# A planner that holds VectorE's work back for GpSimd's casts: linear attention and an expert layer on one core

## The chip, the cores and the metric

One core of one Trainium2 chip runs the kernel. The metric is the device time of one execution in microseconds (us). Each kernel has one profiled execution; of the others only the time, the span and the mean granted clock are on record. SBUF and PSUM are the two memories in which the kernel's tiles lie; its matmuls write PSUM. Engines: PE is TensorE's matmul side, PEld its weight loads, DVE is VectorE, ACT is ScalarE, POOL is GpSimd, SP is SyncE, which here issues loads.

## The reference

```python
def phi(x):                                   # ELU + 1
    return np.where(x > 0, x, np.exp(x) - 1.0) + 1.0
# q, k, v: 8 x 8 x 576 x 64 fp32
kv  = einsum('bhsd,bhse->bhde', phi(k), v);   z   = phi(k).sum(2)
num = einsum('bhsd,bhde->bhse', phi(q), kv);  den = einsum('bhsd,bhd->bhs', phi(q), z) + 1e-6
x = (num / den) transposed and reshaped to 4608 x 512
P = exp(x @ w_gate - max)                     # 8 experts, then 8 rounds of sinkhorn scaling of P
out = sum over e of P[:, e:e+1] * (relu(x @ w1[e]) @ w2[e])      # w1: 512 x 1024, w2: 1024 x 512
```

## The kernel before

The attention is cut into 16 head groups. A group loads k, q and v, casts q and v to fp16 on GpSimd, makes phi of k on ScalarE (exponential) and VectorE (minimum, add, maximum), multiplies kv, transposes q on TensorE, makes phi of q, and then divides, transposes and multiplies on. Matmuls of the first expert fill TensorE between these small steps. This mixed part is called the front here.

No instruction order of the front is written down. Tasks with estimated durations go to a list scheduler inside the kernel, the planner. It picks at every step the task that can start first, and so decides the order on each engine (and for some tasks the engine). In the built program each engine's instructions stand in that fixed order, and those that need another engine's result wait for it by semaphore. Durations in the planner are thus guesses that only shape the order.

```python
class _Plan:
    def add(self, eng, fn, deps=(), prio=0.0, acq=(), use=(), lat=0.0, after=0.0, stall=0.0):
        ...
    def run(self):
        def slot(t):
            r = t["ready"]
            ...                      # and when the buffers that the task takes come free
            return r
        while left:
            ...                      # te, e, t: the task that can start first, and its engine
            t["done"] = te + t["eng"][e] + t["lat"]
            free[e] = te + max(0.0, t["eng"][e] - self.OVER.get(e, 0.0))
            if t["stall"]:
                free["dve"] = max(free["dve"], te) + t["stall"]     # flat charge for a GpSimd cast
            ...
            t["fn"](e)               # emits the instructions

p_in = {n: S_.pool(2) for n in "kvq"}         # two input buffers each for k, q, v
...
def copy(e, dst, src):
    if e == "act":   nc.scalar.copy(out=dst, in_=src)
    elif e == "dve": nc.vector.tensor_copy(out=dst, in_=src)
    else:            nc.gpsimd.tensor_copy(out=dst, in_=src)

# cast of q to fp16 (v likewise)
tqq = fadd(QE[n] if n < 2 else ("pool", 1.2), f_q, ..., stall=QS[n] if n < 2 else 0.35)

def f_m(_):                                    # phi of k on VectorE: the "e" and "tk" instructions
    nc.vector.tensor_scalar(out=ge["tile"], in0=ge["tile"], scalar1=1.0, scalar2=None, op0=ALU.min)
    o = gt["k"]["tile"].rearrange("p j r d -> p r j d")
    if gt["k"]["on"] == "act":
        nc.vector.tensor_tensor(out=o, in0=o, in1=ge["tile"], op=ALU.max)
    else:
        for r in range(2):
            nc.vector.scalar_tensor_tensor(out=o[:, r], in0=gin["k"]["tile"][:, r], scalar=1.0,
                                           in1=ge["tile"][:, r], op0=ALU.add, op1=ALU.max)
tph["k"] = fadd(("dve", 1.35), f_m, deps=[te, tt_], use=[ge, gt["k"], gin["k"]], prio=pr)

def f_qm(_, ...):                              # phi of q on VectorE: the "eq" and "qpT" instructions
    nc.vector.tensor_scalar(out=m, in0=m, scalar1=1.0, scalar2=None, op0=ALU.min)
    nc.vector.scalar_tensor_tensor(out=gq["tile"][...], in0=gp["tile"][...], scalar=1.0,   # gp is in PSUM
                                   in1=m, op0=ALU.add, op1=ALU.max)
tq.append(fadd(("dve", 0.25 + 0.165 * w), f_qm, deps=[t2, tqa], use=[gp, geq, gq], prio=pr))
```

The softmax here doesn't subtract the row's maximum and nothing guards it: scores larger than these inputs give would overflow.

## Time and profile before

| what | before |
|---|---|
| time, median of 3 runs (range) | 985.96 us (984.77 to 986.05) |
| span of the profiled run, its granted clock | 981.6 us, 0.997 (its time was 983.43 us, below all three above) |
| PE busy, idle in the whole span | 964.9 us, 16.7 us |
| PE idle from 20 to 125 us | 5.93 us |
| last logits of the front start at | 138.65 us |
| first matmuls on the gathered rows (xs) start at | 194.76 us |

In the timeline views a line reads: start, length, engine, source line, operation, output<-inputs, shapes, count; in square brackets the idle time of that engine just before, and what ended it.

### The profile page before, as it was taken

The page shows a single profiled execution, that of the slowest core. Times are in us where ns is not written, and L with a number is a line of the kernel's source. Part 1 is how long each engine was busy: PE and PEld are TensorE (multiplying, and loading weights), DVE is VectorE, ACT ScalarE, POOL GpSimd, SP SyncE. Part 2 cuts the span into 40 slices and gives each one's busy share as a digit, 9 for nine tenths or more (in the row PEclk, how much of TensorE's full clock was granted, in tenths as well). Part 3 has the DMA queues.
Part 4 walks back from the last instruction along what each step waited for, and adds up shares of the span by engine and source line. Part 5 has one row for each costly group of instructions (what it writes and reads, how often), then busy time and mean ns, then how long its engine had stood idle before and what let it go on. Part 6 is the DMA issues. An engine that isn't in the chain of part 4 may idle for free.

```text
span 981.6 us, 21435 instructions
## 1 busy us (share of the span) xinstructions
PE 964.9 (98%) x8716; PEld 793.0 (81%) x8716; DVE 767.9 (78%) x1541; ACT 559.6 (57%) x1056; POOL 143.8 (15%) x185
## 2 busy tenths in 40 slices
PE   8998999999999999999999999999999999999997
PEld 4555654488888888888888888888888888888885
DVE  6888788777777777777777777777777777777774
ACT  5787754755555555555555555555555555555552
POOL 5333200001111111111111111111111111111110
PEclk9999999999999999999999999999999999999999
DMA  9976785062226322272226322272225322236654
GB/s 302 308 262 229 224 212 210 1 128 76 74 77 142 96 75 76 75 161 76 76 76 138 100 76 75 77 162 76 76 76 134 104 76 76 76 108 163 161 157 101
DMA packets 47027, 121.98 MB, mean 124 GB/s; under 512 B 4176, under 2 KB 18000, under 8 KB 46928
## 3 DMA queue, kind: packets, MB, share of 16 engines
q1 hardware_dynamic: 32128, 99.76, 30.7%
q0 software_dynamic: 14480, 20.33, 11.6%
q8 instruction: 68, 1.11, 0.5%
q10 hardware_dynamic: 320, 0.52, 0.1%
q14 instruction: 31, 0.25, 0.1%
HBM read 119.69 MB, written 17.69 MB: 140 GB/s over the span
## 4 chain that ended last, share of the span: by engine, by line
PE 89%; DVE 5%; ACT 3%; DMA 2%; issue 1%; SPq 0%; DVEq 0%; ACTq 0%
PE ye L840 33%; PE hq L655 23%; PE att L655 11%; PE Zye L655 6%; PE Zye L840 6%; PE ye L734 4%; PE hq L564 4%; DVE qpT L362 1%; DMA kin<-in_k_dram 1%; DVE tk L300 1%; PE kv_ps L324 1%; DVE eq L361 1%; DMA xd<-xT 1%; PE xt_ps L415 0%; PE num_ps L399 0%
## 5 line engine op out<-in xcount | busy, mean ns | idle before, releaser
L854 DVE SCALAR_TENSOR_TENSOR acc<-ye,P_sb,acc 128x256 f32<-128x256 f32 x620 | 264.6, 476 | 95.2 <-PE ye L840 78.0
L655 PEld LDWEIGHTS <-W 128*128 128x128 f16 x2016 | 197.0, 98 | 23.8
L840 PEld LDWEIGHTS <-S 128*128 128x128 f16 x1984 | 194.1, 98 | 22.5
L840 PE MATMUL ye<-T,S 128*128 128x256 f16 x1488 | 192.9, 273 | 0.0
L864 POOL TENSOR_TENSOR acc<-acc,st 128x256 f32<-128x256 f32 x124 | 87.5, 725 | 625.4 <-ACT st L861 620.5
L681 ACT ACTIVATE h<-hq 128x512 f16<-128x512 f32 x126 | 76.5, 607 | 161.9 <-PE hq L655 161.9
L655 PEld LDWEIGHTS <-w 128*128 128x128 f16 x1512 | 147.5, 98 | 23.3 <-issue 1.0
L840 PEld LDWEIGHTS <-h 128*128 128x128 f16 x1488 | 145.6, 98 | 16.8
L655 PE MATMUL hq<-xs,W 128*128 128x256 f16 x1008 | 151.2, 273 | 0.0
L655 PE MATMUL att<-xs,W 128*128 128x256 f16 x1008 | 151.1, 272 | 0.0
L655 PE MATMUL hq<-xs,w 128*128 128x256 f16 x1008 | 140.8, 272 | 0.8 <-DVE h L684 0.8
L813 DVE TENSOR_TENSOR S<-h 128x1024 f16<-128x1024 f16 x124 | 85.2, 687 | 57.9 <-ACT h L681 57.9
L684 DVE CUSTOM_DVE_ANT_0 h<-att,s 128x512 f16<-128x512 f32 x126 | 86.6, 687 | 13.0 <-ACT s L671 13.0
L861 ACT ACTIVATE st<-Zye,P_sb 128x256 f32<-128x256 f32 x124 | 52.0, 470 | 78.0 <-PE Zye L840 78.0
L671 ACT COPY s<-hq 128x512 f32<-128x512 f32 x126 | 75.1, 596 | 36.8 <-PE hq L655 36.8
L678 ACT ACTIVATE h<-Zye 128x512 f16<-128x512 f32 x126 | 75.2, 597 | 35.1 <-PE Zye L655 35.1
L684 DVE CUSTOM_DVE_ANT_0 h<-hq,s 128x512 f16<-128x512 f32 x126 | 86.4, 686 | 0.1
L667 ACT COPY Zye<-hq 128x512 f32<-128x512 f32 x126 | 73.2, 581 | 17.4 <-PE hq L655 17.4
L734 PE MATMUL ye<-w,h 128*128 128x512 f16 x320 | 77.6, 379 | 0.3 <-DVE acc L225 0.3
L655 PE MATMUL Zye<-xs,w 128*128 128x256 f16 x504 | 75.6, 273 | 0.0
L675 ACT COPY s<-att 128x512 f32<-128x512 f32 x126 | 74.5, 591 | 0.0
L564 PE MATMUL hq<-xT,w 128*128 128x512 f16 x288 | 70.6, 379 | 1.0 <-ACT h L568 0.9
(90 smaller groups left out, 977.9 us busy)
## 6 DMA issues: line engine op xcount, KB each, us to landing
xs<-xd SPq DMA_DIRECT2D x63, 896.0 KB, 4.6
w<-in_moe_w_dram POOLq DMA_DIRECT2D x14, 1024.0 KB, 11.7
out_dram<-acc SPq DMA_DIRECT2D x68, 128.0 KB, 2.4
kin<-in_k_dram SPq DMA_DIRECT2D x14, 576.0 KB, 5.3
qin<-in_q_dram SPq DMA_DIRECT2D x14, 576.0 KB, 6.3
vin<-in_v_dram SPq DMA_DIRECT2D x14, 576.0 KB, 7.7
xd<-xst SPq DMA_DIRECT2D x9, 512.0 KB, 3.2
xd<-xT SPq DMA_DIRECT2D x9, 256.0 KB, 7.4
```

The source lines that it names most:

```text
L564: nc.tensor.matmul(ghq["tile"], lhsT=gw1["tile"][:, c, ts(f, P)], rhs=xT[:, c, ds(512 * g, 512)], start=(c == 0), stop=(c == NDT - 1))
L655: nc.tensor.matmul(dst[:, p, :], lhsT=lhs(p, c), rhs=rhs(c), start=(first and p == 0 and c == 0), stop=(c == 1), skip_group_check=True)
L671: nc.scalar.copy(out=gs2["tile"], in_=gX["tile"])
L675: nc.scalar.copy(out=gs5["tile"], in_=gR["tile"])
L678: nc.scalar.activation(out=hd(0, 0), in_=Zt[1], func=AF.Relu)
L681: nc.scalar.activation(out=hd(1, 0), in_=gX["tile"], func=AF.Relu)
L684: nc.vector._custom_dve(TENSOR_ADD_SAT, out=dst, in0=ps, in1=sb, s0=3.0e38, s1=0.0)
L734: nc.tensor.matmul(gy[tt]["tile"], lhsT=gh["tile"][:, f, ds(P * tt, P)], rhs=gw2["tile"][:, f, :], start=(f == 0), stop=(f == NFT - 1))
L813: nc.vector.tensor_tensor(out=Sx[:, i], in0=a0, in1=a1, op=op)
L840: nc.tensor.matmul(bank(g_)[:, s, :], lhsT=lhs(s, kk), rhs=rhs(kk), start=(new and s == 0 and kk == 0), stop=(kk == 3), skip_group_check=True)
L854: nc.vector.scalar_tensor_tensor(out=dst(), in0=bank(g_)[:, s, :], scalar=P_sb[:, gg, e:e + 1], in1=dst(), op0=ALU.mult, op1=ALU.add)
L864: nc.gpsimd.tensor_tensor(out=dst(), in0=dst(), in1=gst["tile"], op=ALU.add)
```

## The change

The intent: in place of a flat charge to VectorE for every cast on GpSimd, the planner remembers until when the planned cast on GpSimd runs, and makes the VectorE tasks marked `port=True` (phi of k, phi of q, one early cast of q) wait for it. The rest of VectorE's work may be planned under a cast.

What stands behind the mark is seen in the traces as length alone. In the kernel before, from 20 to 150 us, a tk pair takes 1.43 us by itself and 2.28 to 2.39 where casts cover 1.0 us or more of it (0.58 us of cast over one pair left it at 1.43); e takes 0.40 to 0.46 us and, with 0.6 us or more under a cast, 0.91 to 0.97; eq 0.23 to 0.34 us and, with 0.4 us or more, 0.58 to 1.01; tk by maximum 0.76 us and, with 0.9 us or more, 1.53 and 1.59. The qpT instruction, with one input in PSUM, keeps its 0.82 us even where a cast covers all of it. `port` is the planner's name; "the port" stands for this lengthening, and "port-bound" for e, tk and eq.

```diff
-    def add(self, eng, fn, deps=(), prio=0.0, acq=(), use=(), lat=0.0, after=0.0, stall=0.0):
+    def add(self, eng, fn, deps=(), prio=0.0, acq=(), use=(), lat=0.0, after=0.0, lock=False, port=False):
...
+        locked = [0.0]
+
         def slot(t):
-            r = t["ready"]
+            r = max(t["ready"], locked[0]) if t["port"] else t["ready"]
...
-            if t["stall"]:
-                free["dve"] = max(free["dve"], te) + t["stall"]
+            if t["lock"]:
+                locked[0] = t["done"]
...
-        tqq = fadd(QE[n] if n < 2 else ("pool", 1.2), f_q, ..., stall=QS[n] if n < 2 else 0.35)
+        tqq = fadd(QE[n] if n < 2 else ("pool", 1.2), f_q, ..., lock=n > 1 or QE[n][0] == "pool", port=n < 2 and QE[n][0] == "dve")
...
-        tph["k"] = fadd(("dve", 1.35), f_m, ..., prio=pr)
+        tph["k"] = fadd(("dve", 1.35), f_m, ..., prio=pr, port=True)
...        # the cast of v changes as that of q does
-            tq.append(fadd(("dve", 0.25 + 0.165 * w), f_qm, ..., prio=pr))
+            tq.append(fadd(("dve", 0.25 + 0.165 * w), f_qm, ..., prio=pr, port=True))
```

Nothing is added to the program itself: the same work with the same semaphores, in another order. Source lines in the changed kernel are two higher than before (L300 becomes L302).

More of the change, by code (lines that the diff above doesn't have):

```diff
@@ L37, in add @@
         k = len(self.t)
-        t = {"eng": eng, "fn": fn, "prio": prio, "acq": tuple(acq), "lat": lat, "stall": stall, "kids": [], "nd": 0,
+        t = {"eng": eng, "fn": fn, "prio": prio, "acq": tuple(acq), "lat": lat, "lock": lock, "port": port, "kids": [], "nd": 0,
              "ready": after, "done": None, "id": k}
@@ L229 @@
     w_last, in_prev = [None], [None]
-    VE = [("pool", 1.2), ("pool", 1.2)]; VS = [0.9 if x[0] == "pool" else 0.0 for x in VE]
+    VE = [("pool", 1.2), ("pool", 1.2)]
     QT_ATT, QT_HQ = (1,), ()
-    QE = [("dve", 0.75), ("act", 1.17)]; QS = [0.9 if x[0] == "pool" else 0.0 for x in QE]
+    QE = [("dve", 0.75), ("act", 1.17)]
     front_ids = []
@@ L277, in f_q @@
             copy(e, gt["q"]["tile"].rearrange("p j r d -> p r j d"), gin["q"]["tile"])
-        tqq = fadd(QE[n] if n < 2 else ("pool", 1.2), f_q, deps=[tin["q"]], acq=[gt["q"]], use=[gin["q"]], prio=pr, stall=QS[n] if n < 2 else 0.35)
+        tqq = fadd(QE[n] if n < 2 else ("pool", 1.2), f_q, deps=[tin["q"]], acq=[gt["q"]], use=[gin["q"]], prio=pr, lock=n > 1 or QE[n][0] == "pool", port=n < 2 and QE[n][0] == "dve")
         ge = S_.grp(p_e)
@@ L303, in att @@
         tt_ = fadd({"dve": 0.6, "act": 1.17}, f_t, deps=[tin["k"]], acq=[gt["k"]], use=[gin["k"]], prio=pr)
-        tph["k"] = fadd(("dve", 1.35), f_m, deps=[te, tt_], use=[ge, gt["k"], gin["k"]], prio=pr)
+        tph["k"] = fadd(("dve", 1.35), f_m, deps=[te, tt_], use=[ge, gt["k"], gin["k"]], prio=pr, port=True)
         gvv = S_.grp(p_vv)
@@ L313, in att @@
         tvv.append(fadd(VE[n] if n < 2 else ("pool", 1.2), f_v, deps=[ta, tin["v"]],
-                        use=[gvv, gin["v"]], prio=pr, stall=VS[n] if n < 2 else 0.35))
+                        use=[gvv, gin["v"]], prio=pr, lock=n > 1 or VE[n][0] == "pool", port=n < 2 and VE[n][0] == "dve"))
         vcast[n] = tvv[0]
@@ L366, in att @@
             t2 = fadd(("act", 0.2 + 0.09 * w), f_qe, deps=[t1], acq=[geq], use=[gp], prio=pr)
-            tq.append(fadd(("dve", 0.25 + 0.165 * w), f_qm, deps=[t2, tqa], use=[gp, geq, gq], prio=pr))
+            tq.append(fadd(("dve", 0.25 + 0.165 * w), f_qm, deps=[t2, tqa], use=[gp, geq, gq], prio=pr, port=True))
         js = [0, 2, 4, 6, 7]
```

## The prediction

> **What bounds the kernel now.** I read the page first (engine shares and the slices), then the busy time by stretches, then TensorE's own instructions in order of time with the wait before each, then the same view for VectorE and GpSimd side by side. The page says that TensorE is the bound:
>
> ```profile
> PE 964.9 (98%) x8716; PEld 793.0 (81%) x8716; DVE 767.9 (78%) x1541; ACT 559.6 (57%) x1056; POOL 143.8 (15%) x185
> ```
>
> So a change of order can only win what TensorE idles, or lose by making it idle more. Where it idles, the stretches tell (columns: stretch, its length, then busy time and instructions of each engine, granted clock, DMA share, GB/s):
>
> ```profile
> 0.00:20.00 20.00, 15.96 (x124) 7.76 (x125) 12.70 (x26) 9.53 (x17) 10.95 (x18) 0.91 0.95 282
> 20.00:40.00 20.00, 18.37 (x181) 10.80 (x179) 17.45 (x35) 13.48 (x26) 7.64 (x7) 1.00 1.11 334
> 40.00:60.00 20.00, 19.78 (x224) 12.45 (x222) 18.18 (x36) 17.50 (x33) 8.48 (x7) 1.00 0.93 336
> 60.00:80.00 20.00, 19.54 (x245) 12.15 (x243) 16.81 (x34) 15.63 (x31) 5.69 (x5) 1.00 0.64 222
> 80.00:100.00 20.00, 16.93 (x172) 10.06 (x170) 16.67 (x34) 13.65 (x27) 6.06 (x5) 1.00 0.56 185
> 100.00:115.00 15.00, 14.59 (x162) 8.55 (x160) 10.47 (x24) 12.79 (x26) 3.45 (x3) 1.00 0.62 203
> 115.00:125.00 10.00, 9.86 (x136) 6.67 (x134) 9.38 (x21) 6.16 (x13) 3.82 (x4) 1.00 1.09 284
> 125.00:982.00 857.00, 849.89 (x7493) 724.52 (x7490) 666.19 (x1340) 470.84 (x890) 97.68 (x136) 1.00 0.37 104
> ```
>
> The attention part (the front: 16 head groups mixed with matmuls of the first expert) ends at about 138 us, where the last logits run. TensorE idles 4.0 us in the first 20 us (start-up, waiting for the first loads and casts, partly filled with dummy matmuls), then 1.63 + 0.22 + 0.46 + 3.07 + 0.41 + 0.14 = 5.93 us up to 125 us, and from there to 185 us it has no idle time at all. All that this change can reach is thus about 10 us, 1% of the run; a change over 2% is out of reach upwards.
>
> What the change aims at shows in VectorE and GpSimd in order of time (start, length, engine, instruction):
>
> ```profile
> 41.66 1.15 POOL L227 CAST tq<-qin 128x1152 f16<-128x1152 f32 x1 [2.16 <-DMA qin<-in_q_dram]
> 43.08 1.15 POOL L227 CAST vv<-vin 128x1152 f16<-128x1152 f32 x1 [0.27 <-DMA vin<-in_v_dram]
> 95.92 1.46 POOL L227 CAST tq<-qin 128x1152 f16<-128x1152 f32 x1 [3.17 <-PE qt_ps L352]
> ```
>
> ```profile
> 40.22 1.43 DVE L300 SCALAR_TENSOR_TENSOR tk<-kin,e 128x576 f16<-128x576 f32 x2
> 41.98 1.01 DVE L361 TENSOR_SCALAR eq<-eq 128x640 f16<-128x640 f16 x1
> 43.09 0.82 DVE L362 SCALAR_TENSOR_TENSOR qpT<-qt_ps,eq 128x640 f16<-128x640 f16 x1
> 95.62 2.37 DVE L300 SCALAR_TENSOR_TENSOR tk<-kin,e 128x576 f16<-128x576 f32 x2
> ```
>
> The pair of tk halves takes 1.43 us alone and 2.37 us when the cast of 95.92 falls on it. The minimum on eq (0.26 to 0.33 us elsewhere) takes 1.01 us and ends with the cast of 41.66. But the 43.09 instruction, whose one input is in PSUM, keeps its 0.82 us under a whole cast. Summing length minus usual length over the stretched VectorE instructions after 20 us, from the same list: e (usual 0.45) 0.50 + 0.46 + 0.52; tk pair (1.43) 0.85 + 0.96 + 0.94; tk by max (0.76) 0.83 + 0.77; eq (0.28 to 0.32) 0.50 + 0.70 + 0.39 + 0.65 + 0.26. That is 8.3 us of VectorE. TensorE's waits behind it are far smaller:
>
> ```profile
> 29.19 0.67 PE L324 MATMUL kv_ps<-vv,tk 64*128 64x130 f16 x17 [1.16 <-DVE qpT L362]
> 84.40 0.68 PE L324 MATMUL kv_ps<-vv,tk 64*128 64x130 f16 x17 [0.70 <-DVE qpT L362]
> 98.13 0.39 PE L399 MATMUL num_ps<-kvz,qpT 128*128 128x128 f16 x4 [1.25 <-DVE rden L381]
> ```
>
> [...]
>
> **The change part by part.** Every arithmetic result and transfer stays. The old planner charged VectorE a flat 0.35 us for each later cast by GpSimd (28 of them, 9.8 us), whatever VectorE ran. That sum is close to the 8.3 us seen, so the load was right on average; only its place was wrong. The new planner charges nothing flat and holds back marked tasks (phi of k, phi of q, the early q cast) until the planned cast ends, and lets other tasks go first. No wait is added to the program: only order and choice of engine move.
>
> I compared the built programs' instruction order. TensorE, GpSimd and SyncE have the same instructions; TensorE's order differs only from the first groups to the first sinkhorn steps, and GpSimd swaps a few casts. Before the front closes both run 164 first-layer and 144 second-layer matmuls of the first expert, so what follows the close is the same amount of work and the end should move as the close moves. VectorE gains 8 small kvz copies (8 x 0.22 = 1.8 us), one acc copy (0.68) and one group of tk (1.43 in place of 0.76), and loses two xT copies (2 x 0.45): about +2.2 us. ScalarE loses 1.17 + 8 x 0.21 + 0.59 and gains 2 x 0.64: -2.2 us. With VectorE 85% busy between 20 and 125 us (89.0 of 105), 2.2 us more fits only if stretch goes down by as much.
>
> Now the path, wait by wait. First, the start: the new order puts one kvz copy (0.22) and one xT copy (0.45) on VectorE ahead of the second group's last xn, and lets ScalarE do the next exponential (1.18) before its second xT copy. The first real matmuls start at 22.55 us; I put them some 0.5 us later. At the 29.19 wait, VectorE's order (e, tk, eq, qpT, eq, qpT) is unchanged and the casts beside it come when their loads land, so the stretch stays; and 16 instead of 20 first-layer matmuls stand ahead of that kv. Four of 0.216 us are 0.87 us that TensorE now idles there. With 0.3 us of later start: a loss of 1.2 us by 30 us.
>
> Then, waits behind a stretched VectorE: 0.18 (at 45.86), 0.18 (64.80), 0.24 (82.05), 0.70, 1.25, and 0.21 (111.20): 2.76 us. In the new order other work (xn, acc, xT, kvz copies) stands where the port-bound ones stood. I guess three quarters saved: 2.1 us. The waits on ScalarE or on accumulator copies (0.27, 0.30, 0.40, 0.18) are 1.15 us; ScalarE's lighter load may save 0.3. Sum: +1.2 - 2.1 - 0.3 = -1.2 us, so 986.0 becomes 984.8.
>
> **Rivals.** (a) All waits of the front behind VectorE go and nothing is lost at the start: -2.8 - 1.2 = -4.0, about 982. For it: 8.3 us of stretch to save. Against: VectorE gets 2.2 us more, and the first wait's chain is the same. (b) VectorE's stretch falls, but it now idles or runs 2.2 us more while TensorE waits for phi of k held back: a delayed kv takes the place of a stretched one, and the start's loss stays: +1 to +2, about 987. For it: casts are released by landing loads and freed buffers, not by the plan, so a plan exact to a cast's 1.15 us may miss. (c) Nothing: TensorE has enough filler matmuls and each saved wait comes back at the next join; within 0.5 us of 986. The page's 98% speaks for it.
>
> **Range and chances.** The sum of -1.2 us has errors of about 1 us in the start and 1.5 us in the later waits; the three runs of before already span 1.3 us. So 984.8, with 982.3 to 987.3 for 8 in 10. Over 2% is 19.7 us: faster would need twice all reachable idle time, slower a new stall that nothing here suggests. Faster 0.01, within 2% 0.98, slower 0.01.
>
> **What would show it.** In the changed kernel's trace: tk pairs near 1.43 us more often and summed stretch after 20 us well under 8.3 (about 4); the 98.13 and 84.40 waits gone; the kv wait near 29 us longer, near 2 us; first real matmuls near 23 us; the last logits of the front about 1 us before 138.65; from there to the end the same length within 0.5 us. The prediction is wrong if the close moves by more than 3 us, if the time after the close changes, or if stretch falls while TensorE's idle time does not.

## The result, and the profile after

The changed kernel takes 987.95 us (median of 4 runs, 987.58 to 988.7); the kernel before in the same rounds and the earlier ones 985.37 (4 runs, 984.77 to 986.05). The ratio is 1.0027, with a 95% interval of 1.001 to 1.0044. A ratio here is the mean time of one kernel's runs over that of the other's runs of the same rounds, so it is not quite the ratio of the medians. The two are the same within 2%, but the new one is slower, and 987.95 lies above the stated range (982.3 to 987.3).

The page of the changed kernel, engine shares:

```profile
PE 965.3 (98%) x8716; PEld 792.1 (80%) x8716; DVE 770.7 (78%) x1549; ACT 558.0 (57%) x1048; POOL 143.9 (15%) x185
```

TensorE is as busy as before (965.3 against 964.9 us), but the span grew from 981.6 to 985.7: its idle time went from 16.7 to 20.4 us. (The profiles overstate the difference: the profiled execution of before took 983.43 us, 1.9 less than its median, that of the changed kernel 987.82.) Where, the time windows of the changed kernel tell (columns as in the prediction):

```profile
20.00:40.00 20.00, 17.45 (x172) 9.96 (x170) 16.37 (x34) 13.02 (x23) 7.92 (x7) 1.00 1.12 334
40.00:60.00 20.00, 17.21 (x189) 9.99 (x188) 16.96 (x31) 13.04 (x24) 7.02 (x6) 1.00 0.70 245
60.00:80.00 20.00, 18.02 (x175) 10.27 (x172) 16.69 (x33) 14.99 (x27) 5.24 (x5) 1.00 0.60 216
80.00:100.00 20.00, 19.52 (x265) 12.97 (x264) 17.22 (x37) 16.45 (x33) 6.35 (x6) 1.00 0.56 191
100.00:115.00 15.00, 14.35 (x187) 9.34 (x186) 14.17 (x28) 10.93 (x21) 4.63 (x4) 1.00 0.93 319
...
```

Counting also the window that is not shown (115 to 125 us, 9.93 busy), TensorE idles from 20 to 125 us 2.55 + 2.79 + 1.98 + 0.48 + 0.65 + 0.07 = 8.52 us, where it was 5.93. From 80 to 100 us it gained (3.07 to 0.48); from 40 to 60 and from 60 to 80 it lost more (0.22 to 2.79, 0.46 to 1.98). VectorE, which was to be relieved, is busy 1.2 us less from 40 to 60 us, 16.96 for 18.18, just where TensorE waits for it more. TensorE's own instructions in the changed kernel, those with a long wait before them:

```profile
28.66 0.67 PE L326 MATMUL kv_ps<-vv,tk 64*128 64x130 f16 x17 [1.27 <-DVE qpT L364]
...
51.38 0.21 PE L326 MATMUL kv_ps<-vv,tk 64*128 64x130 f16 x1 [0.87 <-DVE qpT L364]
...
52.85 0.69 PE L326 MATMUL kv_ps<-vv,tk 64*128 64x130 f16 x17 [1.25 <-DVE qpT L364]
...
71.14 0.39 PE L401 MATMUL num_ps<-kvz,qpT 128*128 128x128 f16 x4 [0.80 <-DVE rden L383]
72.24 0.28 PE L401 MATMUL num_ps<-kvz,qpT 128*128 128x128 f16 x2 [0.72 <-DVE xn L406]
```

The two waits that the change was to remove, 0.70 us ahead of 84.40 and 1.25 ahead of 98.13, are gone. In their place stand 0.87 + 1.25 us at the kv of group 4 (ahead of its first matmul and of its other 17) and 0.80 + 0.72 at a group's division: 3.64 us for 1.95. The end of the front, in TensorE's timeline, first of the kernel before and then of the changed one:

```profile
138.65 1.04 PE L433 MATMUL lg_ps<-wg_sb,xT 128*128 128x8 f16 x36
...
194.76 0.60 PE L655 MATMUL hq<-xs,w 128*128 128x256 f16 x4
```

```profile
141.81 1.04 PE L435 MATMUL lg_ps<-wg_sb,xT 128*128 128x8 f16 x36
...
198.04 0.60 PE L657 MATMUL hq<-xs,w 128*128 128x256 f16 x4
```

The last logits come 3.16 us later and the first matmuls on gathered rows 3.28 later. From there to the end are 981.6 - 194.8 = 786.8 and 985.7 - 198.0 = 787.7 us. So some 3.2 of the 4.1 us by which the two profiled spans differ are made in the front.

Last, VectorE and GpSimd side by side in the changed kernel:

```profile
42.58 1.27 POOL L229 CAST vv<-vin 128x1152 f16<-128x1152 f32 x1 [0.30 <-PE qt_ps L354]
...
42.88 2.25 DVE L302 SCALAR_TENSOR_TENSOR tk<-kin,e 128x576 f16<-128x576 f32 x2
...
55.82 1.15 POOL L229 CAST tq<-qin 128x1152 f16<-128x1152 f32 x1 [1.00 <-DMA qin<-in_q_dram]
55.92 1.65 DVE L299 TENSOR_TENSOR tk<-tk,e 128x1152 f16<-128x1152 f16 x1
```

The collisions are still there: 2.25 us for the pair that takes 1.43 alone, 1.65 for the maximum that takes 0.76. The casts beside them took 1.27 and 1.15 us, where most take 1.15. Summed as in the prediction, the stretch (the time by which VectorE instructions are lengthened) after 20 us is 8.7 us, where it was 8.3. For the comparisons below I use one fixed sum over all instructions of the five shapes e, tk (two forms) and eq (two forms), from 20 to 150 us, each against the same usual length; it gives 7.6 us before and 8.0 after, and is called the stretch sum. Its level moves by some tenths of a microsecond with the choice of the usual lengths.

Why did the collisions not go? The planner's own times, printed while it plans, give two reasons. The first is that the plan is off:

```
task                          planned start   started on the chip
phi of k, group 4             40.30           42.39
cast of v, group 5            43.43           42.58
cast of q, group 6            47.98           50.71
```

In the plan phi of k of group 4 (to 41.65) is clear of the cast of v, by 1.8 us. On the chip the cast starts 0.85 us earlier than planned and the phi 2.1 us later, so they meet. The rule works with times to a tenth of a microsecond in a plan that is 1 to 3 us off here, and up to 10 us off by the end of the front.

The second reason weighs more: most of the collisions stand in the plan itself. Since only VectorE is held, the planner starts a cast in the middle of a marked task without objection. The planners of both kernels were run again for all 28 casts of groups 2 to 15. In the changed kernel's plan no marked task of these groups starts inside a cast, as the rule demands, but 16 casts start inside a marked task, 7 of them inside phi of k. In the plan of before, 12 of these tasks start inside a cast, and 11 casts inside such a task. In the changed kernel's trace 16 pairs of a cast and a phi overlap in the phi's e, tk or eq by more than 0.1 us; 11 of the 16 overlap in the plan already. The two pairs shown above are among the other five.

### The profile page after: what moved, and what is told of

The parts are those of the page before. It is cut to its first block, busy times and chain, and to the rows that moved or that the text cites. A ratio compares the mean times of both kernels' runs of the same rounds, so it can differ in the third digit from the quotient of the medians.

```text
span 985.7 us, 21428 instructions
## 1 busy us (share of the span) xinstructions
PE 965.3 (98%) x8716; PEld 792.1 (80%) x8716; DVE 770.7 (78%) x1549; ACT 558.0 (57%) x1048; POOL 143.9 (15%) x185
## 4 chain that ended last, share of the span: by engine, by line
PE 90%; DVE 7%; ACT 2%; issue 1%; DMA 0%; DVEq 0%; ACTq 0%
PE ye L842 33%; PE hq L657 23%; PE att L657 11%; PE Zye L657 6%; PE Zye L842 5%; PE ye L736 5%; PE hq L566 4%; DVE qpT L364 1%; DVE xn L406 1%; DVE tk L302 1%; PE kv_ps L326 1%; DVE tk L299 1%; DVE eq L363 1%; PE num_ps L401 1%; PE xt_ps L417 1%
```

## The experiments

The theory from the two traces was: the collisions are not what changed; the new order holds phi back, has its own waits, and these are the 3 us. Rivals: the stretch itself costs more where it now falls; the transposes of q take, ahead of a kv, the two PSUM buffers that it needs ("banks"); single held-back phis are to blame and can be moved; late k loads; or the whole is chance, since any change of a number in the planner gives another order. Eighteen kernels were run. Two of them give a wrong result; the others are correct.

**1 and 2. Both orders with hardly any cast.** Casts on GpSimd of groups 2 to 15 do 2 of 64 columns. The result is wrong; the order is untouched.

```diff
+            w = 2 if len(tiny) > 1 else src.shape[-1]
+            tiny.append(1)
-            nc.gpsimd.tensor_copy(out=dst, in_=src)
+            nc.gpsimd.tensor_copy(out=dst[:, :, :, 0:w], in_=src[:, :, :, 0:w])
```

> The changed kernel with its order untouched, but GpSimd's casts of groups 2 to 15 copy 2 of each 64 columns (wrong result on purpose)[...]. Theory A (the new order itself keeps TensorE waiting[...]): it stays 2 to 3 us slower than the same edit of the kernel before. Theory B (same quality of order, but casts now fall on worse VectorE instructions): it comes within 0.7 us of that. Both expect stretch near 0 and a time below 987.95.

> The kernel before with the same shortened casts (wrong result on purpose). It gives the most that any avoidance of the port could win: if the port's cost on TensorE is the 2.8 us that I counted, about 982.5; if TensorE's filler hides it, 984 to 985.

Measured: the changed kernel 983.62 us (ratio to before 0.9982, 0.9971 to 0.9994), the kernel before 980.44 (0.9952, 0.994 to 0.9964), with before at 985.04 in the same job. The stretch sum falls to nothing in both (-0.6 and -0.8; below zero, since the usual lengths are a little long). The order's difference stays: 983.62 - 980.44 = 3.2 us, where with casts it was 987.95 - 985.37 = 2.6. The casts cost about as much under either rule: 985.04 - 980.44 = 4.6 us before, 987.95 - 983.62 = 4.3 after; these are upper bounds for what the collisions cost, since the shorter cast itself also ends sooner. In the changed order without casts the new waits are still there:

```profile
50.78 0.21 PE L330 MATMUL kv_ps<-vv,tk 64*128 64x130 f16 x1 [0.74 <-DVE qpT L368]
51.78 0.69 PE L330 MATMUL kv_ps<-vv,tk 64*128 64x130 f16 x17 [0.79 <-DVE qpT L368]
69.53 0.28 PE L405 MATMUL num_ps<-kvz,qpT 128*128 128x128 f16 x2 [0.68 <-DVE xn L410]
```

That is 2.21 us where it was 3.64, with nothing stretched. They belong to the order. In the kernel before without casts, no wait of 0.4 us behind VectorE is left from 20 to 145 us. (TensorE's idle time in these two profiles, 4.98 and 4.61 us from 22 to 150 us, doesn't show the 3.2: the profiled run of before without casts was its slowest, 982.07 against 979.95 to 980.61, and has 1.55 + 0.82 us of waits for weights in it. So the 3.2 us rest on the timings, whose ranges do not touch; the waits show where such a difference can stand, not its sum.)

**3 and 4. The two halves of the change.** The first drops the flat charge and holds nothing back; the second holds back and charges as well.

```diff
 # neither (f_qm likewise)
-tph["k"] = fadd(("dve", 1.35), f_m, ..., prio=pr, port=True)
+tph["k"] = fadd(("dve", 1.35), f_m, ..., prio=pr)
 # both
 if t["lock"]:
     locked[0] = t["done"]
+    free["dve"] = max(free["dve"], te) + 0.35
```

> The changed kernel with the flat charge gone but nothing held back[...]. If dropping the 0.35 us charge per cast is what hurts (VectorE planned too light), it is as slow as the changed kernel or slower, 988 or more. If holding back phi of k and phi of q hurts, it comes back to about 985.5.

> The changed kernel with the flat charge of 0.35 us per cast put back beside the holding. If the lost charge hurts, about 985.5; if the holding hurts, 988 or more (VectorE is then charged twice).

Measured: neither 988.49 (1.003, 1.0018 to 1.0042), both 990.28 (1.0046, 1.0032 to 1.006); each has one half-clock dip of 1.7 us in its profile, of the kind described with runs 13 to 16. With the charge alone (before, 985.37) and the hold alone (after, 987.95) all four combinations are there, one order each: by the time, the charge alone is best. By the front it looks different. The first matmuls on gathered rows start at 195.19 us with both and at 194.76 with the charge alone, but at 198.04 with the hold alone and at 199.55 with neither (1.7 of it the dip). What "both" loses, it loses after the front: TensorE waits 1.16 us for ScalarE ahead of 207.10 and 2.83 ahead of 215.44, and its dip stands there. So the traces point to the lost charge more than to the hold. As other experiments show, one order of a rule is a draw with a spread of several us, so four orders do not divide the cost between the two.

**5. The transposes of group 5 behind the kv of groups 4 and 5.** The recorded order of the changed kernel is replayed task for task (a replay without moves gives identical instruction lists), with three things of group 5 moved: its transposes, exponentials and phi of q.

```diff
 # the recorded task list
-qt5 qe5 ... kv4 kv5 ... qm5
+kv4 kv5 z4 z5 qt5 qe5 ... xn4 qm5
```

> The changed kernel's order replayed instruction for instruction, with one thing moved: the transposes of group 5's q with their exp and phi go behind the kv matmuls of groups 4 and 5, as they stand in the kernel before. Bank theory (held-back phi of q 4 lets the transposes of q 5 take the two PSUM banks that kv 4 needs, 0.87 + 1.25 us of TensorE's idle time): about 2 us under the changed kernel, 985.9. Rival (TensorE meets the same VectorE load at the next join): within 0.7 us of 988.

Measured: 987.74 (1.0027, 1.0015 to 1.0039): 1.8 us above the bank theory's figure, and where the rival put it. The waits at the kv of group 4 went, and in their place came, in TensorE's timeline of this run:

```profile
52.44 0.38 PE L613 MATMUL den_ps<-kvz,qpT 128*128 128x2 f16 x9 [0.33 <-DVE kvz L463]
...
59.27 0.69 PE L562 MATMUL kv_ps<-vv,tk 64*128 64x130 f16 x17 [1.01 <-DVE qpT L600]
```

with smaller ones of 0.28 to 0.29 us ahead of 51.23, 58.05 and 61.46. The next groups pay. This does not clear the PSUM buffers: the waits at group 4 did go with the transposes, but these now stand ahead of the kv of group 6, and its 17 matmuls wait for the second phi of q of group 5 in the same way (the 1.01 us). The bank theory of the one wait fits; that its removal wins time does not.

**6. Also phi of k of group 8 behind the division of group 6.**

```diff
-... m8 ... xn6 ...
+... xn6 m8 ...
```

> The same, and phi of k of group 8 goes behind the division of group 6, which waited behind it (TensorE idle 0.80 + 0.72 us at 71 to 72 us). If each such wait is lost time: another 1 to 1.5 us less, about 984.5. If the waits come back elsewhere: as the run with the first move.

Measured: 988.65 (1.0035, 1.0022 to 1.0049): 4.2 us above the hope; the rival, waits that come back, had it about right. The waits at the division went and two others came, one of 0.86 us ahead of 79.40 and this one:

```profile
74.92 0.40 PE L590 MATMUL qt_ps<-ident,tq 128*128 128x128 f16 x4 [1.73 <-DVE qpT L600]
```

**7. The order of before, phi of k of groups 10 and 12 held back by hand.** This is the improvement for which the change was made: the two waits at 84.40 and 98.13 of before removed and nothing else, by moving one phi of k ahead of each to after the division that it delayed.

> The kernel before, its order replayed, with two moves on VectorE alone: phi of k of groups 10 and 12 go behind the phi of q and the divisions that waited for them (TensorE idle 0.24 + 0.70 and 1.25 us). If TensorE's waits in the front are lost time one for one, 2.2 us under the kernel before, about 982.9. If they come back: within 0.7 us of it.

Measured: 989.47 (987.88 to 992.57; ratio 1.0047, 1.0031 to 1.0063): 6.6 us above the first expectation, and above the second as well. The two waits went, as planned. What came are two waits of the same kind, 2.44 and 2.37 us long, on TensorE (ahead of 88.56 and 113.41) and two of 10.40 and 10.64 us on GpSimd; the first of each, in the timelines of this run:

```profile
88.56 0.17 PE L611 MATMUL den_ps<-kvz,qpT 128*128 128x2 f16 x1 [2.44 <-ACT kvz L459]
```

```profile
96.70 1.15 POOL L463 CAST vv<-vin 128x1152 f16<-128x1152 f32 x1 [10.40 <-DMA vin<-in_v_dram]
```

Phi of k is the last reader of the k input buffer, and there are two. Held back, it frees the buffer late: the k loads of groups 12 and 14 were issued at 88.14 and 106.57 us in place of 81.97 and 98.05. The loads of q and v stand behind that of k in SyncE's order (in this run at 88.60 and 89.11 us, after 88.14), so the casts of both waited, and the stream of the later groups with them. A phi with slack, off the critical path itself, still sets when the next loads start. Something else came with the two long waits: in the profiled execution (992.57 us, the slowest) a dip of the granted clock follows each, 0.68 + 1.00 and 0.76 + 0.96 us of lost clock, 3.4 us in all; such dips are described with runs 13 to 16. The other executions have no such record, so their part in the 6.6 us is not shown.

**8 to 12. Is it the order or the rule?** Four other values of the planner's numbers (the flat charge 0.40 or 0.30 for 0.35, the told length of a cast 1.15 or 1.25 for 1.2) give other orders of the same rule. And one run keeps the changed order but lets GpSimd yield on the chip: before each cast it reads 64 columns of the latest phi's output, so that a cast cannot start inside a phi.

```diff
+            if lastp[0] is not None:                       # set by f_m and f_qm
+                nc.gpsimd.tensor_copy(out=junk, in_=lastp[0])
             nc.gpsimd.tensor_copy(out=dst, in_=src)
```

> The kernel before with its flat charge at 0.40 us in place of 0.35, nothing else. If the order of the kernel before owes its time to that charge being right on average, within 1 us of 985.0. If it owes it to one lucky order among many (its transposes of q 5 again stand ahead of kv 4 here), 987 to 990 as the three re-made orders measured so far.

> The old rule with its charge at 0.30 us in place of 0.35. If the old rule is the better one, 984 to 986, as at 0.35 and 0.40. If orders are draws, 984 to 990.

> The new rule unchanged, but the planner is told that a cast takes 1.15 us (as the trace has it) and not 1.2: a control for chance. If the rule itself costs 2.6 us, 987 to 989. If each re-made order is a draw from a spread of some 2 us either way, it may come out anywhere from 984 to 990.

> The same control to the other side, 1.25 us: 987 to 989 if the rule costs, 984 to 990 if the order is a draw.

> The changed kernel, same order on every engine; before each GpSimd cast GpSimd also reads 64 columns that the latest phi task ahead of it in the plan has written, so it can't start a cast before that task is done, as the plan assumes. If the change fails because casts start earlier on the chip than planned[...]: summed stretch from 8.7 to under 4 us and the time to 985 or less. If the order itself is at fault: stretch falls, time within 1 us of 988 or above, since casts come later.

Measured, charge 0.40: 984.98 (0.9998, 0.9986 to 1.001). Charge 0.30: 981.57 (0.9953, 0.9934 to 0.9972). Cast told as 1.15: 987.21 (1.001, 0.9989 to 1.003). Told as 1.25: 984.96 (0.999, 0.997 to 1.0009). Yielding: 986.88 (1.0008, 0.999 to 1.0027). All but the first of these shared one job, which was noisy: the kernel before lay between 983.4 and 989.26 in it, so their intervals are wide.

The yield did what it was made for: the stretch sum fell from 8.0 to 4.0. It adds on the chip the direction that the planner's rule lacks. What it was worth is at most about 987.95 - 986.88 = 1.1 us (across two jobs, whose ranges touch), and TensorE's idle time from 22 to 150 us even stayed (8.36 for 8.09). The tk pair just ahead of the kv, at 50.90, takes its plain 1.43 us and the kv waits still. TensorE's timeline of the yielding run:

```profile
53.58 0.21 PE L332 MATMUL kv_ps<-vv,tk 64*128 64x130 f16 x1 [0.95 <-DVE qpT L370]
54.58 0.69 PE L332 MATMUL kv_ps<-vv,tk 64*128 64x130 f16 x17 [0.79 <-DVE qpT L370]
```

**13 to 16. More draws of each rule,** to tell the rule from chance: the cast told as 1.18 and 1.22, the charge at 0.37 and 0.25.

> Another draw of the new rule, a cast told as 1.18 us. Rule costs: 987 to 989. Draws: 984 to 990.

> Another draw of the new rule, 1.22 us. Rule costs: 987 to 989. Draws: 984 to 990.

> Another draw of the old rule, charge 0.37 us. Old rule better by itself: 982 to 986. Draws: 982 to 990.

> Another draw of the old rule, charge 0.25 us. Old rule better by itself: 982 to 986. Draws: 982 to 990.

Measured: 995.46 (1.0106, 1.0092 to 1.0119), 993.3 (1.0085, 1.0071 to 1.0099), 982.79 (0.9978, 0.9964 to 0.9993), 982.8 (0.9978, 0.9966 to 0.9991). All draws together; the idle column is 128 us less TensorE's busy time from 22 to 150 us:

| rule | told | median us | stretch sum us | PE idle 22 to 150 us |
|---|---|---|---|---|
| flat charge | 0.25 | 982.8 | 8.8 | 4.78 |
| flat charge | 0.30 | 981.57 | 7.0 | 5.34 |
| flat charge (before) | 0.35 | 985.37 | 7.6 | 5.64 |
| flat charge | 0.37 | 982.79 | 7.7 | 4.84 |
| flat charge | 0.40 | 984.98 | 8.7 | 6.81 |
| hold, no charge | cast 1.15 | 987.21 | 8.0 | 9.20 |
| hold, no charge | cast 1.18 | 995.46 | 8.2 | 14.02 |
| hold, no charge (after) | cast 1.20 | 987.95 | 8.0 | 8.09 |
| hold, no charge | cast 1.22 | 993.3 | 7.8 | 12.43 |
| hold, no charge | cast 1.25 | 984.96 | 8.5 | 6.45 |

The means are 983.5 us for the flat charge and 989.8 for the hold. Of 25 pairs, 23 have the hold above the charge. The mean stretch sum is 8.0 us for the charge and 8.1 for the hold. So the new rule (the hold in place of the charge) reaches nothing of what it is for on average, and makes slower orders: 4.6 us more of TensorE idle time in the mean (10.0 against 5.5), most of the 6.3 us. The worst draw shows the kinds of wait it makes, in TensorE's timeline for the cast told as 1.18:

```profile
54.05 0.69 PE L326 MATMUL kv_ps<-vv,tk 64*128 64x130 f16 x17 [1.70 <-DVE qpT L364]
...
112.92 0.44 PE L417 MATMUL xt_ps<-ident,xn 128*128 128x128 f16 x5 [1.80 <-DVE xn L406]
...
132.55 0.38 PE L377 MATMUL den_ps<-kvz,qpT 128*128 128x2 f16 x9 [2.93 <-ACT kvz L225]
```

And it shows where most of the rest is. The time windows of the same run right after the first of these waits (the third number from the end is the granted clock):

```profile
54.00:56.00 2.00, 1.95 (x27) 1.16 (x28) 0.45 (x2) 0.93 (x3) 1.13 (x1) 0.82 1.03 381
56.00:58.00 2.00, 2.00 (x36) 1.78 (x33) 1.56 (x5) 1.11 (x4) 0.14 (x2) 0.50 0.89 305
```

The granted clock falls to half (0.50 from 56 to 58 us), while TensorE has work without a gap (2.00 us busy of 2.00). Summed over slices of 4 us, (1 - clock) x 4 comes to 0.36 + 1.36 = 1.72 us there, as half speed for 3.44 us would give. The other two waits are followed by the same, 1.36 + 0.36 and 1.12 + 0.60. The cast told as 1.22 has two such dips, 3.4 us, after waits of 1.75 and of 0.94 + 1.83 us; the other eight draws of the table have none from 20 to 960 us. (A dip between 8 and 16 us, during the start-up, stands in 11 of the 20 profiles, of both rules; TensorE is busy 2.0 to 3.9 us in its slices of 4.) In all 20 profiles there are ten dips between 20 and 960 us, of 1.68 to 1.72 us each. Each stands in the 4 us slice in which a TensorE wait ends or in the next one, and these waits are from 0.56 us (run 3, ahead of 111.75) to 2.93 us long. But the 0.87 + 1.25 us of the changed kernel have no dip behind them, while the 0.86 + 0.78 us of run 17 at the same kv do. So these traces do not tell which waits a dip follows. In the profiled executions a dip costs its full size: the start of the first matmuls on gathered rows, less TensorE's idle time since 20 us, less the dips, is 187.3 to 188.7 us in the five profiles with a dip in the front and 186.9 to 188.8 in the others. So the two outliers are waits plus dips. As an estimate, if the dips of the profiled execution stand in the median one too, 995.46 - 5.2 and 993.3 - 3.4 would both be near 990, and without the dips the means of the rules still differ by 6.3 - (5.2 + 3.4) / 5 = 4.6 us, about the idle time. (It is not sure that they do: the execution of 993.3 us has a mean clock of 0.998 over its span of 991.5 us; two dips of 1.7 us would alone bring it to 0.997.) The pair of kernels has no dip in the profiled front after 20 us, so its difference there is idle time alone.

A caution goes with the table: one number told differently is one draw, and the told number differs in kind between the rules. That the single pair of kernels differs by just 2.6 us is chance within that spread; that it differs upwards is what 23 of the 25 pairs do. The ten draws set hold without charge against charge without hold, so they do not tell the two apart either.

**17 and 18. Are late k loads the cause?** In the changed kernel the k loads of groups 10 and 11 are issued at 71.06 and 80.73 us, in the kernel before at 67.29 and 69.87; run 7 had shown that a late k load can cost much. A third k buffer, under the two recorded orders, takes this dependence away. Room was made by cutting a constant tile of zeros from 512 to 64 columns, read repeatedly.

```diff
-gr["tile"] = fp.tile([P, 2, NJ, D], FP32, tag=nm + "in", name=nm + "in", bufs=2)
+gr["tile"] = fp.tile([P, 2, NJ, D], FP32, tag=nm + "in", name=nm + "in", bufs=3 if nm == "k" else 2)
```

> The order of the changed kernel replayed task for task, with nothing else changed but a third buffer for the k input (the room is made by cutting the constant zero tile of the warm-up matmuls from 512 to 64 columns, read repeatedly). Load theory (the new rule holds phi of k back, which frees the two k buffers late, so that loads, casts and everything behind them come late): the load of k no longer waits for phi of k, k loads of groups 6 to 13 are issued 3 us or more earlier than in the changed kernel (59.43, 71.06, 80.73, 97.74), and the time falls from 987.9 to 984 to 985.5. Rival (the waits come from the order in which PE, VectorE and ScalarE take their work, and the loads are late beside it): loads earlier, time stays at 987 to 988.5.

> The control: the order of the kernel before, replayed task for task, with the same third k buffer and the same cut of the zero tile. Load theory: here phi of k frees the buffers early already, so the time gains at most 1 us: 984 to 985.4. Rival: also 984.5 to 986; what tells them apart is the difference between the two orders, which is 2.6 us with two buffers: the load theory expects under 1.2 us with three, the rival 2 to 3 us.

Measured: the changed order 991.13 (1.006, 1.0046 to 1.0073), the order of before 988.84 (1.0037, 1.0024 to 1.0049), before itself 985.29. All the absolute numbers expected were missed: both orders lost over 3 us. The difference between the orders, 991.13 - 988.84 = 2.3 us, lies in the rival's 2 to 3; but the profile of the changed order has a half-clock dip of 1.7 us in it (after the waits near 55) and that of the other none, so this difference does not settle the size. What the traces do show is that the loads came earlier and the waits stayed. SyncE's issues and TensorE's timeline of the changed order with three buffers:

```profile
62.64 0.37 SPq L504 DMA_DIRECT2D kin<-in_k_dram  x1
...
74.16 0.37 SPq L504 DMA_DIRECT2D kin<-in_k_dram  x1
```

```profile
54.52 0.21 PE L562 MATMUL kv_ps<-vv,tk 64*128 64x130 f16 x1 [0.86 <-DVE qpT L600]
55.52 0.69 PE L562 MATMUL kv_ps<-vv,tk 64*128 64x130 f16 x17 [0.78 <-DVE qpT L600]
...
74.23 0.39 PE L637 MATMUL num_ps<-kvz,qpT 128*128 128x128 f16 x4 [0.77 <-DVE rden L619]
75.34 0.28 PE L637 MATMUL num_ps<-kvz,qpT 128*128 128x128 f16 x2 [0.72 <-DVE xn L642]
```

The k loads of groups 10 and 11 are 8.4 and 6.6 us earlier, and the same four waits sum to 3.13 us, where they were 3.64. So these waits do not hang on late loads, though in run 7 late loads were a real cost. As to the loss that both runs share: the k load of group 4 went from about 26 to about 13 us, in among the weight loads, and TensorE of the order of before waited for weights:

```profile
36.27 1.89 PE L970 MATMUL ye<-w,h 128*128 128x512 f16 x8 [1.73 <-DMA w<-in_moe_w_dram]
```

and 0.86 us more ahead of 41.94, besides 1.60 us for a cast of q ahead of 26.25. That may be where the loss came from; it is not shown, since two-buffer profiles have waits for weights too (run 2: 1.55 + 0.82). What the loads cost the changed kernel in time is left open by these runs.

**A version that beats both kernels** is the old rule with a charge of 0.30, above: 981.57 us (980.59 to 982.73) against 985.72 for before in the same job. It is the best of ten measured orders, so part of the gain may be luck; its neighbours 0.25 and 0.37, at 982.8, are also faster than before.

## Why the prediction was wrong

- **The bound and the reach were right.** TensorE's work did not move (964.9 and 965.3 us), all but 0.9 us of the difference was made in the front, and the change stayed far within 2%.
- **The start was over-estimated.** The first real matmuls came at 22.67 us (22.55 before; 23 was said), and the wait ahead of the kv near 29 us grew from 1.16 to 1.27, not to about 2. A loss of 1.2 us was booked and about 0.2 was there: four matmuls fewer do stand ahead of that kv, but VectorE's chain of phi of q, unchanged in order, ended 0.5 us earlier (the 17 matmuls start at 28.66 for 29.19). This error worked against the one below.
- **The work moved about as counted:** VectorE +2.8 us on the page (+2.2 was said), ScalarE -1.6 (-2.2).
- **The step that failed** is "I guess three quarters saved: 2.1 us", with the stretch falling to about 4 us. The named waits at 84.40 and 98.13 did go, but the stretch stayed at 8.7 us. The premise, "In the new order other work (xn, acc, xT, kvz copies) stands where the port-bound ones stood", holds only in part, in the plan already: the hold keeps a marked task from starting inside a cast, but not a cast from starting inside a marked task, and 16 of 28 casts are planned so. 11 of the 16 collisions on the chip were in the plan. For the rest the plan's times are off, by 0.85 to 2.7 us in the three tasks compared; this objection I had written down under rival (b), the one-sided rule I had not seen.
- **The missing term** is the price of the order itself. The sum had only savings and the start in it, as if the marked work could be put later for nothing. Without casts the new order is still 3.2 us slower than the old one, and waits of 0.74, 0.79 and 0.68 us stand in it with nothing stretched. So -2.1 for the later waits should have been about +2.4 by the medians, +3.0 by the close of the front in the profiles. That close moved by 3.16 us, past the 3 us that the prediction had named as a sign of being wrong. Rival (b), "a delayed kv takes the place of a stretched one", said "about 987" and named the right place: the two largest new waits are at one kv, that of group 4. Its account was right in part. The stretch did not fall, the start's loss was not there, and the kv did not wait for its phi of k, which had ended at 45.13, but for the phi of q of group 5 (qpT, to 51.33 and 52.80), whose transposes held its PSUM buffers.
- **Saved waits come back.** Rival (c) was right in this: each hand-made removal (runs 5, 6 and 7) took its wait away and gained nothing.
- **Even full success would have been worth less than the stretch.** With the casts all but gone the kernels gained 4.3 to 4.6 us for 8 us of stretch; halving the stretch gave about 1.1 at most.

What stays open: how the cost divides between the hold on phi of k, the hold on phi of q and the lost flat charge; whether a rule that also holds casts back behind marked tasks would lower the stretch and the time, which no run tests in the planner; and which property of an order makes the spread of several us between draws of one rule. The stretch sum does not follow the time in the table, moving single waits did not help, and the share of late k loads is not settled.

## What to carry to other kernels

A rule that holds one side back leaves the collisions that the other side starts: before building, count in the plan itself how many are left (here 16 casts of 28). Even then a static plan avoids a collision only if its times are right to less than the collision lasts (here casts of 1.15 us, and starts off by 0.85 to 2.7 us). Here a charge that was right on average did as well against the collisions as the one-sided hold (mean stretch sum 8.0 and 8.1 us), and gave faster orders (983.5 and 989.8 us). Before crediting a new schedule, price the order without the conflict (here by shrinking the casts), and compare several draws of each rule: five orders of one rule spread from 981.57 to 985.37 us and five of the other from 984.96 to 995.46, and one planner number nudged by 2% (1.20 to 1.18) moved the time by 7.5 us. Work with slack is not free to move if it is the last reader of a load's buffer (in run 7 the next k loads came 6.2 and 8.5 us later).
